# The first tile of an attention and two-expert-layer kernel: its distances, bias and operand parts cut into what the first scores read and the rest

## The chip, the cores and the metric

The kernel runs on one core of one Trainium2 chip. The metric is the device time of one execution in microseconds (us). The engines are named as the profile names them: PE (TensorE matmul), PEld (its weight loads), DVE (VectorE), ACT (ScalarE), POOL (GpSimd) and SP (SyncE, which issues the transfers here).

## What is computed

Attention over 2 batches, 8 heads, 768 positions and head size 64, then two layers of experts over the 1536 rows that come out. The part that matters here is the attention:

```python
scores = scale * np.matmul(q, k.transpose(0, 1, 3, 2))
is_global = pos[None, :] < int(n_global)            # 8
is_local = (rel >= 0) & (rel < int(n_local))        # 96, rel = row - column
keep = is_global | is_local
dist = np.where(is_global & ~is_local, float(n_local), np.abs(rel))
bias = -slopes[:, None, None] * dist[None, :, :]
scores = np.where(keep, scores + bias[None], -1e9)
a = np.exp(scores - max); a = a / (sum + 1e-9)
return np.matmul(a, v)
# then: top-1 of 8 experts (moe), then a mixture of 4 experts (moe2)
```

A row attends to at most 96 positions behind it and to the 8 global ones, so a tile of 128 rows needs its own 128 columns and those of the tile ahead of it.

## The kernel before

**Tiles and units.** The 1536 rows are 12 tiles of 128. A unit `u` is one tile with four of its eight heads, so there are 24 units; tile 0 is units 0 and 1. The loop over `u` (L483) runs several stages of different units in one turn: `stage_qk(u + 2)` (the scores on PE), `stage_e(u + 1)` (exponentials on ACT), `stage_t(u)` (transposes on PE), `stage_s(u + 2)` (scores plus bias and the row minimum on DVE, tiles `sc0x`, `sc1x`, ...), `stage_pv(u - 1)` (weights times values on PE). The order on each engine is the order of the code (`manual_schedule`); nothing is reordered.

**High and low parts.** A float32 product is made of three fp32r matmuls: high by high, high by low, low by high. So each tile's q and k get a high part (`xq00x` or `xq10x`, `kh`) by a copy on ACT (on POOL for `kh` from tile 2 on), and a low part (`xq01x` or `xq11x`, `kl`) by a subtraction in the helper `sub_lo` (L68), on POOL for q, on DVE for k of tiles 0 and 1. `prep_q`, `prep_k` do this for whole tiles of 512 columns. `save_gk` copies the global keys (`gk`) on POOL.

**Distances and bias.** `rel`, `key` and `far` are bf16 scratch rows of 640 columns inside the tile `xr` (the profile calls them `xr`): columns 0 to 511 serve tiles with a tile ahead of them, columns 512 to 639 serve a first tile, which has only its own 128 columns. POOL fills them (L135 to L142). DVE makes the distance from them with four instructions (L306 to L309) once the two integers `nints` have landed, and `make_bias` multiplies it by each head's slope (L330): first columns 512 to 639 for 8 heads, then, in the turn `u == -1`, columns 0 to 511 for 8 heads.

**PE's accumulators and fillers.** The scores of a unit take two of three PSUM tiles in turn: unit 0 `pa2x` and `pa3x`, unit 1 `sps` and `pa2x`, unit 2 `pa3x` and `sps`, unit 3 `pa2x` and `pa3x`. A unit's scores can be written when `stage_s` has read what stood there before. `warm` puts filler matmuls on a zero tile ahead of the first four units' scores, 2, 6, 6 and 6 of them, behind the 24 of L315.

**Transfers.** SP issues the loads in the order of the code: `nints`, the q half and the k half of tile 0 (`qk0x`), tile 1 (`qk1x`), small ones, then tile 2 into `qk0x` when its last reader is done.

Of the kernel before, what the change touches and what calls it, by code (L numbers as in the profile page):

```python
# [8 lines left out]
F32 = mybir.dt.float32  # L9
# [4 lines left out]
AF = mybir.ActivationFunctionType  # L14
ALU = mybir.AluOpType
# [24 lines left out]
FAR = float(4 * NOVF)  # L40
BIG = float(2 ** 38)
# [3 lines left out]
def attention_moe_moe(ctx: ExitStack, tc: tile.TileContext, qkv, nints_d, wg, w1, w2, dprob, u1, u2, out):  # L45
    nc = tc.nc
# [6 lines left out]
    cp = ctx.enter_context(tc.tile_pool(name="cp", bufs=1))  # L53
# [13 lines left out]
    def sub_lo(eng, lo, src, hi):  # L67
        eng.tensor_tensor(out=lo, in0=src, in1=hi.bitcast(F32), op=ALU.subtract)  # L68
# [50 lines left out]
    xq = [[wxp.tile([P, ND, P], F32R, name=f"xq{n}{m}x") for m in range(2)] for n in range(2)]  # L119
# [9 lines left out]
    ident = cp.tile([P, P], F32, name="ident")  # L129
# [1 line left out]
    xr = cp.tile([P, NT, D], F32, name="xr")  # L131
    nc.vector.memset(xr[:, NT - 1, :], 0.0)
    rel, key, far = (xr[:, n, :].bitcast(BF16)[:, 0:W] for n in range(NT - 4, NT - 1))
    for c, n, step, off in ((512, 1, 0, 0), (0, 2, 256, P)):
        nc.gpsimd.iota(rel[:, c:c + n * 256 - (P if n == 1 else 0)], pattern=[[0, n], [-1, 256 if n == 2 else P]], base=off, channel_multiplier=1,  # L135
                       allow_small_or_imprecise_dtypes=True)
        nc.gpsimd.iota(key[:, c:c + n * 256 - (P if n == 1 else 0)], pattern=[[0, n], [1, 256 if n == 2 else P]], base=0, channel_multiplier=0,
                       allow_small_or_imprecise_dtypes=True)
    for c in (512, 128, 384):
        nc.gpsimd.affine_select(out=rel[:, c:c + P], in_=rel[:, c:c + P], pattern=[[-1, P]], compare_op=ALU.is_ge, fill=1024.0,  # L140
                                base=0, channel_multiplier=1)
    nc.gpsimd.memset(rel[:, 256:256 + GMAX], 1024.0)  # L142
    rowf = cp.tile([P, 1], F32, name="rowf")
    nc.gpsimd.iota(rowf, pattern=[[0, 1]], base=0, channel_multiplier=1, allow_small_or_imprecise_dtypes=True)
    colf = cp.tile([P, 256], F32, name="colf")
    nc.gpsimd.iota(colf, pattern=[[1, 256]], base=0, channel_multiplier=0, allow_small_or_imprecise_dtypes=True)
    make_identity(nc, ident)
    tri = cp.tile([P, P], BF16, name="tri")
    ones = cp.tile([P, P], BF16, name="ones")
    nc.vector.memset(ones, 1.0)  # L150
    base = cp.tile([P, E1], F32, name="base")
# [134 lines left out]
        sub_lo(nc.vector, lo, src, hi)  # L286

    qkr = [lp.tile([P, 2, 512], F32, name=f"qk{j}x") for j in range(2)]
    for c in range(2):
        nc.sync.dma_start(qkr[0][:, c], qkv[0, :, c])  # L290
    load_qk(1)
    nc.sync.dma_start(wgt, wg)
# [5 lines left out]
    nval = cp.tile([P, 2], F32, name="nval")  # L298
    nc.vector.scalar_tensor_tensor(out=nval, in0=neg, scalar=float(2 ** 32), in1=nf[:, :, 0], op0=ALU.mult, op1=ALU.add)
    ngv, nlv = nval[:, 0:1], nval[:, 1:2]  # L300
    okt = cp.tile([P, 2], F32, name="okt")
    nc.vector.tensor_scalar(out=okt[:, 0:1], in0=nlv, scalar1=1.0, scalar2=None, op0=ALU.is_ge)
    nc.vector.scalar_tensor_tensor(out=okt[:, 1:2], in0=nlv, scalar=float(P - GMAX + 1), in1=okt[:, 0:1], op0=ALU.is_le, op1=ALU.mult)
    bad = cp.tile([P, 2], F32, name="bad")
    nc.vector.scalar_tensor_tensor(out=bad[:, 0:1], in0=ngv, scalar=float(GMAX), in1=okt[:, 1:2], op0=ALU.is_le, op1=ALU.mult)
    nc.vector.tensor_scalar(out=far, in0=rel, scalar1=nlv, scalar2=BIG, op0=ALU.is_ge, op1=ALU.mult)  # L306
    nc.vector.tensor_scalar(out=key, in0=key, scalar1=ngv, scalar2=BIG, op0=ALU.is_ge, op1=ALU.mult)
    nc.vector.tensor_tensor(out=rel, in0=far, in1=rel, op=ALU.max)
    nc.vector.scalar_tensor_tensor(out=rel, in0=key, scalar=nlv, in1=rel, op0=ALU.max, op1=ALU.min)  # L309
    nc.vector.tensor_scalar(out=tri, in0=colf[:, 0:P], scalar1=rowf, scalar2=None, op0=ALU.is_gt)  # L310
    nc.vector.tensor_scalar(out=base, in0=colf[:, 0:E1], scalar1=float(P), scalar2=-FAR, op0=ALU.mult, op1=ALU.add)
    with tc.tile_pool(name="ps_w", bufs=1, space=PSUM) as ps_w:
        wt = ps_w.tile([P, 256], F32, name="wt")
        for n in range(NWARM):
# [2 lines left out]
    with ExitStack() as c2:  # L317
# [7 lines left out]
        a3 = c2.enter_context(tc.tile_pool(name="a3", bufs=4))  # L325
        bias = bp.tile([P, H, W], BF16, name="bias")

        def make_bias(c):
            for h in range(H):
                nc.vector.tensor_scalar(out=bias[:, h, c], in0=rel[:, c], scalar1=-8.0 * 2.0 ** -(h + 1), scalar2=None, op0=ALU.mult)  # L330

        kh = bp.tile([P, 3, NPAIR, P], F32R, name="kh")
# [26 lines left out]
        def prep_q(t):  # L359
            qs[t] = qh, ql = xq[t % 2]  # L360
            raw = qkr[t % 2][:, 0].rearrange("p (d t) -> p d t", d=NPAIR)
            nc.scalar.activation(out=qh, in_=raw, func=AF.Copy)
            sub_lo(nc.gpsimd, ql, raw, qh)

        def prep_k(t):
            so = t % 3
            raw = qkr[t % 2][:, 1].rearrange("p (d t) -> p d t", d=NPAIR)
            if t < 2:
                nc.scalar.activation(out=kh[:, so], in_=raw, func=AF.Copy)
            else:  # L370
                copy_g(kh[:, so], raw)
            sub_lo(nc.vector if t < 2 else nc.gpsimd, kl[:, so], raw, kh[:, so])

        def save_gk(t):
            so = t % 3
# [4 lines left out]
        def load_v(t):  # L380
            nc.sync.dma_start(vv[:, t % 4, :, 0:HD], qkv[t, :, 2].rearrange("p (h e) -> p h e", h=H))
# [92 lines left out]

        NU = 2 * NT
        load_v(0)
        nc.gpsimd.memset(vv[:, :, :, HD:HV], 1.0)
        prep_q(0)
        prep_k(0)
        save_gk(0)  # L480
        load_qk(2)
        make_bias(slice(512, 640))
        for u in range(-2, NU + 5):  # L483
            t, g = divmod(u, 2)
            if u < 2:
                warm(WARMS[u + 2])
            if u + 2 < NU:
                stage_qk(u + 2)
            if 0 <= u - 2 < NU:
                run(norm(u - 2))  # L490
            if g == 0:
                if 0 <= t - 2 < NT:
                    run(rts[t - 2]["steps"][0])
                if t + 1 < NT and t >= 0:
                    load_v(t + 1)
                if t in (0, NI):
                    load_gv(t)
# [112 lines left out]
    with ExitStack() as c2:  # L610
# [76 lines left out]
        for e in range(E1 - 1):  # L687
# [17 lines left out]
            hs = hidden(pl, mp)  # L705
# [460 lines left out]
```

## Time and profile before

| | |
|---|---|
| median of 3 runs | 754.18 us (754.17 to 754.35) |
| the profiled execution: its own time, its span | 756.36 us, 754.6 us |
| PE busy over the span | 736.4 us, 98% |
| DVE, ACT, POOL busy | 522.1 us (69%), 312.7 us (41%), 252.8 us (33%) |
| granted TensorE clock, mean | 0.984 |
| first scores on DVE (unit 0), first of unit 2, first of unit 3 | 10.88 us, 17.09 us, 19.25 us |

The span runs from the first to the last instruction; 1.8 us of the profiled execution lie around it. A share of busy time is a mean over stages: in the first 20 us, which is where the change lies, PE waits for DVE, and afterwards PE has work almost without a gap. The granted clock is a share of full speed (2.4 GHz): 0.50 is the lower of its two levels, 1.2 GHz.

### The profile page before, as it was taken

What the parts mean: (1) busy time and instruction counts of PE and PEld (TensorE: products, weight loads), DVE (VectorE), ACT (ScalarE), POOL (GpSimd) and SP (SyncE); (2) the same over time, 40 slices, a digit from 0 to 9 for tenths busy, and PEclk for the clock granted to TensorE, in tenths of its full rate; (3) what the DMA queues carried; (4) which work ended last, traced back from release to release, by engine and by line L of the source; (5) the groups of instructions that cost most, each with busy time, mean ns of one, the idle gap of its engine ahead of it and who ended that gap; (6) DMA issues with size and microseconds to landing.
All of it is one profiled execution on the core that took longest, in us unless ns stands there. A gap on an engine that the chain in (4) does not pass through costs nothing.

```text
span 754.6 us, 12189 instructions
## 1 busy us (share of the span) xinstructions
PE 736.4 (98%) x4794; PEld 657.3 (87%) x4794; DVE 522.1 (69%) x1024; ACT 312.7 (41%) x489; POOL 252.8 (33%) x244
## 2 busy tenths in 40 slices
PE   8999998999999999999999999999999999999996
PEld 7999997777777898899999999999999999999995
DVE  7777863678769888576666666676666666666665
ACT  4878861687855544513223132232222322213110
POOL 5666631000046604724414244141341523415000
PEclk8999996999999999999999999999999999999999
DMA  6867602999931300200001000010000100011013
GB/s 163 277 220 247 215 21 86 387 364 405 342 103 54 99 16 28 84 29 29 29 29 56 29 29 29 29 56 29 30 29 29 56 28 29 34 38 43 1 43 129
DMA packets 36018, 74.87 MB, mean 99 GB/s; under 512 B 15960, under 2 KB 16216, under 8 KB 35954
## 3 DMA queue, kind: packets, MB, share of 16 engines
q1 hardware_dynamic: 34034, 69.39, 26.7%
q0 software_dynamic: 1920, 4.64, 1.9%
q8 instruction: 39, 0.64, 0.3%
q14 instruction: 25, 0.20, 0.1%
HBM read 65.19 MB, written 10.49 MB: 100 GB/s over the span
## 4 chain that ended last, share of the span: by engine, by line
PE 87%; DVE 5%; DMA 3%; issue 2%; ACT 2%; POOL 0%; POOLq 0%; ACTq 0%; DVEq 0%
PE pf L110 6%; PE pf L109 6%; PE pf L111 6%; PE pg L109 4%; PE pg L110 4%; PE pg L111 4%; PE pa0x L111 3%; PE pa0x L109 3%; PE pa1x L110 3%; PE pa0x L110 3%; PE pa1x L109 3%; PE pa3x L109 3%; PE pa3x L111 3%; PE pa1x L111 3%; PE pa3x L110 3%; PE pa2x L111 3%
## 5 line engine op out<-in xcount | busy, mean ns | idle before, releaser
L914 DVE TENSOR_TENSOR cc<-pg,sf 128x768 f32<-128x768 f32 x48 | 45.9, 957 | 57.0 <-PE pg L111 55.6
L896 ACT ACTIVATE sf<-pf 128x768 f32<-128x768 f32 x48 | 39.0, 813 | 107.5 <-PE pf L111 107.5
L938 ACT ACTIVATE hh0x<-cc 128x1024 fp32r<-128x1024 f32 x24 | 25.5, 1060 | 120.5 <-DVE cc L923 117.8
L938 ACT ACTIVATE hh1x<-cc 128x1024 fp32r<-128x1024 f32 x23 | 24.4, 1060 | 106.6 <-DVE cc L923 106.6
L599 POOL TENSOR_TENSOR w6x<-w4x 128x256 f32<-128x256 f32 x8 | 9.4, 1178 | 175.1 <-DMA w4x<-in_u_dram 93.2
L923 DVE TENSOR_TENSOR cc<-cc,uv 128x768 f32<-128x768 f32 x47 | 52.5, 1117 | 1.6
L939 DVE SCALAR_TENSOR_TENSOR hl0x<-cc,hh0x 128x1024 fp32r<-128x1024 f32 x24 | 29.5, 1231 | 24.8 <-ACT hh0x L938 24.8
L939 DVE SCALAR_TENSOR_TENSOR hl1x<-cc,hh1x 128x1024 fp32r<-128x1024 f32 x23 | 28.5, 1241 | 25.0 <-ACT hh1x L938 25.0
L897 DVE TENSOR_TENSOR uv<-pf,sf 128x256 f32<-128x256 f32 x48 | 20.4, 424 | 34.1 <-ACT sf L896 34.1
L110 PE MATMUL pf<-xl,r8x 128*128 128x256 f32 x144 | 40.8, 283 | 2.7 <-DVE xl L68 2.5
L857 DVE SCALAR_TENSOR_TENSOR xr<-pa2x,pr,xr 128x512 f32<-128x512 f32 x44 | 33.0, 750 | 13.4 <-PE pa2x L111 13.4
L109 PE MATMUL pf<-xh,r8x 128*128 128x256 f32 x144 | 40.6, 282 | 0.0
L111 PE MATMUL pf<-xh,r6x 128*128 128x256 f32 x144 | 40.4, 281 | 0.0
L109 PE MATMUL pf<-xh,r14x 128*128 128x256 f32 x144 | 40.4, 281 | 0.0
L110 PE MATMUL pf<-xl,r14x 128*128 128x256 f32 x144 | 40.4, 281 | 0.0
L111 PE MATMUL pf<-xh,r12x 128*128 128x256 f32 x144 | 40.4, 281 | 0.0
L599 POOL TENSOR_TENSOR w12x<-w10x 128x256 f32<-128x256 f32 x8 | 8.9, 1119 | 92.6 <-DMA w10x<-in_u_dram 92.6
L857 DVE SCALAR_TENSOR_TENSOR xr<-pa1x,pr,xr 128x512 f32<-128x512 f32 (+1 forms) x46 | 33.9, 737 | 2.2 <-PE pa1x L111 2.2
L857 DVE SCALAR_TENSOR_TENSOR xr<-pa0x,pr,xr 128x512 f32<-128x512 f32 (+1 forms) x46 | 33.9, 736 | 1.2 <-PE pa0x L111 1.2
L857 DVE SCALAR_TENSOR_TENSOR xr<-pa3x,pr,xr 128x512 f32<-128x512 f32 x45 | 33.5, 744 | 0.6 <-PE pa3x L111 0.6
L110 PEld LDWEIGHTS pf<-xl,r8x 128*128 128x128 f32 x144 | 27.0, 188 | 3.4 <-issue 2.5
L68 POOL TENSOR_TENSOR r11x<-w11x,r15x 128x1024 fp32r<-128x1024 f32 x7 | 17.0, 2424 | 35.8 <-ACT r15x L97 35.8
(1189 smaller groups left out, 2700.2 us busy)
## 6 DMA issues: line engine op xcount, KB each, us to landing
w4x<-in_u_dram SPq DMA_DIRECT2D x8, 512.0 KB, 3.2
w5x<-in_u_dram SPq DMA_DIRECT2D x8, 512.0 KB
w10x<-in_u_dram SPq DMA_DIRECT2D x8, 512.0 KB, 3.9
w11x<-in_u_dram SPq DMA_DIRECT2D x8, 512.0 KB, 3.4
qk1x<-in_qkv_dram SPq DMA_DIRECT2D x6, 512.0 KB, 4.7
vv<-in_qkv_dram SPq DMA_DIRECT2D x12, 256.0 KB, 4.9
out_dram<-xr SPq DMA_DIRECT2D x11, 256.0 KB, 2.0
qk0x<-in_qkv_dram SPq DMA_DIRECT2D x5, 512.0 KB, 4.2
```

The lines of the kernel that those rows point to most:

```text
L68: eng.tensor_tensor(out=lo, in0=src, in1=hi.bitcast(F32), op=ALU.subtract)
L109: nc.tensor.matmul(o, ah, bh, start=start, stop=False)
L110: nc.tensor.matmul(o, ah, bl, start=False, stop=False)
L111: nc.tensor.matmul(o, al, bh, start=False, stop=stop)
L599: eng.tensor_tensor(out=sm[:, 0], in0=a21, in1=a22, op=ALU.add)
L857: nc.vector.scalar_tensor_tensor(out=acc[:, tt, cs], in0=ac[:, cs], scalar=pr[:, tt, e:e + 1], in1=acc[:, tt, cs], op0=ALU.mult, op1=ALU.add)
L896: nc.scalar.activation(out=sf, in_=pf[:, 0:3], func=AF.Copy)
L897: tt(out=uv, in0=pf[:, 3], in1=sf[:, 0], op=ALU.add)
L914: tt(out=cc[:, 0:3], in0=pg, in1=sf, op=ALU.add)
L923: tt(out=cc[:, 1:4], in0=cc[:, 1:4], in1=uv.unsqueeze(1).to_broadcast([P, 3, 256]), op=ALU.add)
L938: nc.scalar.activation(out=hh, in_=cc, func=AF.Relu)
L939: nc.vector.scalar_tensor_tensor(out=hl, in0=cc, scalar=0.0, in1=hh.bitcast(F32), op0=ALU.max, op1=ALU.subtract)
```

## The change

It reorders and cuts up the work of tile 0; the sum of what is computed stays. (1) POOL fills columns 512 to 639 first, then makes `ident`, then the other columns. (2) The k half of tile 0 is loaded ahead of the q half. (3) The four distance instructions become a function `window(c)`, called for columns 512 to 639 ahead of the first scores and for columns 0 to 511 in the turn `u == -1`. (4) `prep_first` makes the high and low parts of tile 0 in two halves of two head pairs: for the first half the low parts of k and q are subtracted on DVE, for the second half both on POOL. (5) The bias of columns 512 to 639 is made for heads 0 to 3 ahead of the first scores and for heads 4 to 7 behind them. (6) Five small instructions (`okt`, `bad`, `tri`, `base`) move behind the first scores.

```diff
-    for c, n, step, off in ((512, 1, 0, 0), (0, 2, 256, P)):
...
-    for c in (512, 128, 384):
+    iotas(512, 1)
+    past_only(512)
+    make_identity(nc, ident)
...
-    make_identity(nc, ident)
+    iotas(0, 2)
+    for c in (128, 384):
+        past_only(c)
...
-    for c in range(2):
+    for c in (1, 0):
         nc.sync.dma_start(qkr[0][:, c], qkv[0, :, c])
...
+    def window(c):
+        nc.vector.tensor_scalar(out=far[:, c], in0=rel[:, c], scalar1=nlv, scalar2=BIG, op0=ALU.is_ge, op1=ALU.mult)
+        nc.vector.tensor_scalar(out=key[:, c], in0=key[:, c], scalar1=ngv, scalar2=BIG, op0=ALU.is_ge, op1=ALU.mult)
+        nc.vector.tensor_tensor(out=rel[:, c], in0=far[:, c], in1=rel[:, c], op=ALU.max)
+        nc.vector.scalar_tensor_tensor(out=rel[:, c], in0=key[:, c], scalar=nlv, in1=rel[:, c], op0=ALU.max, op1=ALU.min)
...
-        def make_bias(c):
-            for h in range(H):
+        def make_bias(c, hs=range(H)):
+            for h in hs:
...
+        def prep_first():
+            raws = [qkr[0][:, n].rearrange("p (d t) -> p d t", d=NPAIR) for n in (1, 0)]
+            qs[0] = xq[0]
+            for d in (slice(0, 2), slice(2, 4)):
+                eng = nc.gpsimd if d.start else nc.vector
+                parts = [(kh[:, 0, d], kl[:, 0, d], raws[0][:, d]), (xq[0][0][:, d], xq[0][1][:, d], raws[1][:, d])]
+                for hi, _, raw in parts:
+                    nc.scalar.activation(out=hi, in_=raw, func=AF.Copy)
+                for hi, lo, raw in parts:
+                    sub_lo(eng, lo, raw, hi)
...
         load_v(0)
+        window(slice(512, 640))
         nc.gpsimd.memset(vv[:, :, :, HD:HV], 1.0)
-        prep_q(0)
-        prep_k(0)
+        prep_first()
+        make_bias(slice(512, 640), range(4))
         save_gk(0)
         load_qk(2)
-        make_bias(slice(512, 640))
...
             if u == -2:
+                make_bias(slice(512, 640), range(4, H))
+                small_constants()
                 prep_q(1)
...
             if u == -1:
+                window(slice(0, 512))
                 make_bias(slice(0, 512))
```

What stands on DVE ahead of the first scores (`sc0x`), behind `nval` (the two integers as floats), in the kernel before:

```order
L302 TENSOR_SCALAR okt<-nval 128x1
L303 SCALAR_TENSOR_TENSOR okt<-nval,okt 128x1
L305 SCALAR_TENSOR_TENSOR bad<-nval,okt 128x1
L306 TENSOR_SCALAR xr<-xr,nval 128x640
L307 TENSOR_SCALAR xr<-xr,nval 128x640
L308 TENSOR_TENSOR xr<-xr 128x640
L309 SCALAR_TENSOR_TENSOR xr<-xr,nval 128x640
L310 TENSOR_SCALAR tri<-colf,rowf 128x128
L311 TENSOR_SCALAR base<-colf 128x8
L68 TENSOR_TENSOR kl<-qk0x,kh 128x512
L330 TENSOR_SCALAR bias<-xr 128x128 x8
L418 ISA sc0x,mn<-pa2x,bias 128x128
```

and in the change:

```order
L311 TENSOR_SCALAR xr<-xr,nval 128x128
L312 TENSOR_SCALAR xr<-xr,nval 128x128
L313 TENSOR_TENSOR xr<-xr 128x128
L314 SCALAR_TENSOR_TENSOR xr<-xr,nval 128x128
L68 TENSOR_TENSOR kl<-qk0x,kh 128x256
L68 TENSOR_TENSOR xq01x<-qk0x,xq00x 128x256
L342 TENSOR_SCALAR bias<-xr 128x128 x4
L442 ISA sc0x,mn<-pa2x,bias 128x128
```

Five small instructions, four of eight bias instructions and the 512 other columns have left this place; half of the q subtraction has come to it.

What stands on DVE from the last scores of unit 1 (`sc1x`) to the first of unit 2 (`sc2x`), in the kernel before:

```order
L418 ISA mn 128x1
L418 ISA sc1x,mn<-pa2x,bias 128x128
L418 ISA mn 128x1
L330 TENSOR_SCALAR bias<-xr 128x512 x8
L418 ISA sc2x,mn<-pa3x,bias 128x256
```

and in the change:

```order
L442 ISA mn 128x1
L311 TENSOR_SCALAR xr<-xr,nval 128x512
L312 TENSOR_SCALAR xr<-xr,nval 128x512
L313 TENSOR_TENSOR xr<-xr 128x512
L314 SCALAR_TENSOR_TENSOR xr<-xr,nval 128x512
L342 TENSOR_SCALAR bias<-xr 128x512 x8
L442 ISA sc2x,mn<-pa3x,bias 128x256
```

The four distance instructions of the 512 columns now stand ahead of unit 2's scores. Between the scores of units 0 and 1 DVE has, besides the subtraction of tile 1's `kl` that was there, four bias instructions and the five small ones. So all that left the place ahead of `sc0x` stands ahead of `sc2x` still.

POOL's subtractions and copies for tiles 0, 1 and 2, in the kernel before (`qk0x` holds tile 0, then tile 2):

```order
L68 TENSOR_TENSOR xq01x<-qk0x,xq00x 128x512
L378 TENSOR_SCALAR gk<-kh 128x128
L378 TENSOR_SCALAR gk<-kl 128x128
L68 TENSOR_TENSOR xq11x<-qk1x,xq10x 128x512
L357 TENSOR_SCALAR kh<-qk0x 128x512
L68 TENSOR_TENSOR kl<-qk0x,kh 128x512
L68 TENSOR_TENSOR xq01x<-qk0x,xq00x 128x512
```

and in the change:

```order
L68 TENSOR_TENSOR kl<-qk0x,kh 128x256
L68 TENSOR_TENSOR xq01x<-qk0x,xq00x 128x256
L402 TENSOR_SCALAR gk<-kh 128x128
L402 TENSOR_SCALAR gk<-kl 128x128
L68 TENSOR_TENSOR xq11x<-qk1x,xq10x 128x512
L369 TENSOR_SCALAR kh<-qk0x 128x512
L68 TENSOR_TENSOR kl<-qk0x,kh 128x512
L68 TENSOR_TENSOR xq01x<-qk0x,xq00x 128x512
```

One subtraction of 512 columns has become two of 256. PE's matmuls stand in the same order in both.

## Rows read from the trace of the kernel before

**Rows 1.** The page: granted TensorE clock in 40 slices of the span, in tenths.
```profile
PEclk8999996999999999999999999999999999999999
```

**Rows 2.** Timeline of DVE: start, duration, instruction, idle before it and who ended that.
```profile
4.47 0.15 DVE L302 TENSOR_SCALAR okt<-nval 128x1 f32<-128x1 f32 x1
...
4.93 0.38 DVE L306 TENSOR_SCALAR xr<-xr,nval 128x640 bf16<-128x640 bf16 x1
...
5.52 1.58 DVE L308 TENSOR_TENSOR xr<-xr 128x640 bf16<-128x640 bf16 x1
7.13 0.89 DVE L309 SCALAR_TENSOR_TENSOR xr<-xr,nval 128x640 bf16<-128x640 bf16 x1
...
8.80 2.16 DVE L330 TENSOR_SCALAR bias<-xr 128x128 bf16<-128x128 bf16 x8
10.88 0.28 DVE L418 CUSTOM_DVE_ANT_0 sc0x<-pa2x,bias 128x128 f32<-128x128 f32 x1
...
11.72 0.68 DVE L68 TENSOR_TENSOR kl<-qk1x,kh 128x512 fp32r<-128x512 f32 x1
13.04 0.29 DVE L418 CUSTOM_DVE_ANT_0 sc1x<-sps,bias 128x128 f32<-128x128 f32 x1 [0.63 <-PE sps L407]
...
13.89 3.28 DVE L330 TENSOR_SCALAR bias<-xr 128x512 bf16<-128x512 bf16 x8
17.09 0.41 DVE L418 CUSTOM_DVE_ANT_0 sc2x<-pa3x,bias 128x256 f32<-128x256 f32 x1
```

**Rows 3.** Timeline of POOL.
```profile
5.47 1.28 POOL L68 TENSOR_TENSOR xq01x<-qk0x,xq00x 128x512 fp32r<-128x512 f32 x1 [1.33 <-ACT xq00x L362]
...
8.97 0.42 POOL L378 TENSOR_SCALAR gk<-kl 128x128 fp32r<-128x128 f32 x1 [1.71 <-DVE kl L68]
9.36 1.34 POOL L68 TENSOR_TENSOR xq11x<-qk1x,xq10x 128x512 fp32r<-128x512 f32 x1
12.53 0.62 POOL L357 TENSOR_SCALAR kh<-qk0x 128x512 fp32r<-128x512 f32 x1 [1.83 <-DMA qk0x<-in_qkv_dram]
...
14.47 1.33 POOL L68 TENSOR_TENSOR xq01x<-qk0x,xq00x 128x512 fp32r<-128x512 f32 x1
```

**Rows 4.** The tile `bias`, 8.5 to 11 us: count, duration ns min/median/max.
```profile
L330 DVE TENSOR_SCALAR bias<-xr x8: 181/188/1303, 8.8 to 10.8; 128x128 bf16<-128x128 bf16 x8
```

**Rows 5.** Timeline of DVE, the second of the eight bias instructions of 512 columns.
```profile
14.60 1.36 DVE L330 TENSOR_SCALAR bias<-xr 128x512 bf16<-128x512 bf16 x1
```

**Rows 6.** Timeline of ACT.
```profile
4.75 0.63 ACT L362 ACTIVATE xq00x<-qk0x 128x512 fp32r<-128x512 f32 x1 [2.52 <-DMA qk0x<-in_qkv_dram]
5.42 0.63 ACT L369 ACTIVATE kh<-qk0x 128x512 fp32r<-128x512 f32 x1
```

**Rows 7.** Timeline of SP's transfers.
```profile
8.95 0.34 SPq L276 DMA_DIRECT2D qk0x<-in_qkv_dram  x1
```

**Rows 8.** Timeline of PE: first scores of unit 0, second matmul of unit 3.
```profile
6.95 0.32 PE L407 MATMUL pa2x<-kh,xq00x 64*128 64x128 f32 x1
...
18.25 0.38 PE L407 MATMUL pa3x<-kh,xq10x 64*128 64x256 f32 x1
```

**Rows 9.** Busy time by stretch: length, each engine (count), granted clock, DMA share, GB/s.
```profile
7.00:8.90 1.90, 0.27 (x3) 0.13 (x2) 1.86 (x6) 1.02 (x2) 0.26 (x1) 1.00 0.28 42
...
10.20:11.60 1.40, 1.11 (x5) 0.69 (x3) 1.40 (x10) 0.40 (x2) 0.50 (x1) 0.50 0.70 260
11.60:13.10 1.50, 1.46 (x11) 1.35 (x11) 0.87 (x4) 0.92 (x5) 0.57 (x1) 0.50 0.16 63
13.10:16.90 3.80, 3.80 (x22) 3.34 (x22) 3.80 (x16) 1.76 (x5) 2.62 (x3) 0.50 0.90 229
17.00:47.00 30.00, 30.00 (x296) 28.33 (x295) 22.09 (x122) 23.95 (x55) 18.98 (x28) 1.00 0.83 252
```

**Rows 10.** Busy time by stretch at the end of the attention.
```profile
109.10:112.50 3.40, 2.57 (x25) 2.57 (x24) 1.50 (x11) 1.13 (x3) 1.75 (x3) 1.00 0.05 15
...
122.80:126.20 3.40, 3.40 (x19) 3.34 (x19) 0.76 (x6) 0.00 (x0) 1.19 (x2) 0.50 0.04 15
```

More of the change, by code (lines that the diff above doesn't have):

```diff
@@ L133, in attention_moe_moe, with iotas, past_only @@
     rel, key, far = (xr[:, n, :].bitcast(BF16)[:, 0:W] for n in range(NT - 4, NT - 1))
-    for c, n, step, off in ((512, 1, 0, 0), (0, 2, 256, P)):
[L135 to L138, printed above, removed]
-    for c in (512, 128, 384):
+    def iotas(c, n):
+        w = 256 if n == 2 else P
+        for a, step, off, ch in ((rel, -1, P if n == 2 else 0, 1), (key, 1, 0, 0)):
+            nc.gpsimd.iota(a[:, c:c + n * w], pattern=[[0, n], [step, w]], base=off, channel_multiplier=ch, allow_small_or_imprecise_dtypes=True)
+    def past_only(c):
         nc.gpsimd.affine_select(out=rel[:, c:c + P], in_=rel[:, c:c + P], pattern=[[-1, P]], compare_op=ALU.is_ge, fill=1024.0,
                                 base=0, channel_multiplier=1)
-    nc.gpsimd.memset(rel[:, 256:256 + GMAX], 1024.0)
+    iotas(512, 1)
+    past_only(512)
+    make_identity(nc, ident)
     rowf = cp.tile([P, 1], F32, name="rowf")
@@ L146, in attention_moe_moe @@
     nc.gpsimd.iota(colf, pattern=[[1, 256]], base=0, channel_multiplier=0, allow_small_or_imprecise_dtypes=True)
-    make_identity(nc, ident)
+    iotas(0, 2)
+    for c in (128, 384):
+        past_only(c)
+    nc.gpsimd.memset(rel[:, 256:256 + GMAX], 1024.0)
     tri = cp.tile([P, P], BF16, name="tri")
@@ L300, in attention_moe_moe, with small_constants @@
     ngv, nlv = nval[:, 0:1], nval[:, 1:2]
-    okt = cp.tile([P, 2], F32, name="okt")
-    nc.vector.tensor_scalar(out=okt[:, 0:1], in0=nlv, scalar1=1.0, scalar2=None, op0=ALU.is_ge)
-    nc.vector.scalar_tensor_tensor(out=okt[:, 1:2], in0=nlv, scalar=float(P - GMAX + 1), in1=okt[:, 0:1], op0=ALU.is_le, op1=ALU.mult)
     bad = cp.tile([P, 2], F32, name="bad")
[L305 to L311, printed above, removed]
+    def window(c):
[3 more added lines that the diff above has]
+        nc.vector.scalar_tensor_tensor(out=rel[:, c], in0=key[:, c], scalar=nlv, in1=rel[:, c], op0=ALU.max, op1=ALU.min)
+    def small_constants():
+        okt = cp.tile([P, 2], F32, name="okt")
+        nc.vector.tensor_scalar(out=okt[:, 0:1], in0=nlv, scalar1=1.0, scalar2=None, op0=ALU.is_ge)
+        nc.vector.scalar_tensor_tensor(out=okt[:, 1:2], in0=nlv, scalar=float(P - GMAX + 1), in1=okt[:, 0:1], op0=ALU.is_le, op1=ALU.mult)
+        nc.vector.scalar_tensor_tensor(out=bad[:, 0:1], in0=ngv, scalar=float(GMAX), in1=okt[:, 1:2], op0=ALU.is_le, op1=ALU.mult)
+        nc.vector.tensor_scalar(out=tri, in0=colf[:, 0:P], scalar1=rowf, scalar2=None, op0=ALU.is_gt)
+        nc.vector.tensor_scalar(out=base, in0=colf[:, 0:E1], scalar1=float(P), scalar2=-FAR, op0=ALU.mult, op1=ALU.add)
     with tc.tile_pool(name="ps_w", bufs=1, space=PSUM) as ps_w:
```

## Prediction

> **What bounds the kernel now.** I looked first at what PE does, since it is busy 98% of the span, and in which stretches that is not true. The table by stretch shows it: from 17 to 47 us PE has 30.00 of 30 us of work, but from 7.0 to 8.9 us only 0.27 of 1.90 [rows 9]. So the fill of the pipeline, up to some 18 us, is the only part that the change touches, and whatever PE gets there earlier or later is carried behind it. What PE waits for in the fill is read from two places. Its first scores start at 6.95 us; the second matmul of unit 3 starts at 18.25 us [rows 8], and it needs `pa3x`, which DVE frees when it has read unit 2's heads 0 and 2. DVE starts on unit 2 at 17.09 us, straight behind the eight bias instructions of 512 columns [rows 2]. From 18.25 us on PE never waits for long. **So unit 2's scores on DVE, not unit 0's, are the gate of the fill**, and the question is where DVE comes to them.
>
> **What DVE does until then.** From 4.47 to 17.09 us are 12.62 us, and much of it is not work. A bias instruction of 128 columns takes 188 ns, but one takes 1303 ns [rows 4]; it is the one that runs while POOL subtracts `xq11x` (9.36 to 10.70 us). The TENSOR_TENSOR at 5.52 us takes 1.58 us and ends 0.35 us after POOL's `xq01x` (5.47 to 6.75 us); the second wide bias instruction takes 1.36 us beside POOL's third subtraction (14.47 to 15.80 us) [rows 2, 3, 5]. The eight narrow ones need 0.10 us each without that, from start to start, and took 2.08 us. So a DVE instruction that meets a two-input subtraction on POOL stands until POOL is through. The Trainium skill, page "SBUF — State Buffer", section "Who interferes with whom", has this as a lock on a port pair that VectorE and GpSimd share: whichever issues first keeps the other out for the whole instruction. The trace agrees, with 1303 ns against 188; by that rule unit 2 starts where the sum below has it, and if the three long instructions were chance, it would start where the second rival has it.
>
> **The change on DVE, step by step.** The unhindered prices, start to start, from [rows 2, 4, 5]: a distance TENSOR_SCALAR of 640 columns 0.30 us (two from 4.93 to 5.52), so some 0.13 and 0.25 for 128 and 512; the TENSOR_TENSOR 0.35 us at 640 (its part behind POOL), so 0.2 and 0.35 with a wait for its input; the SCALAR_TENSOR_TENSOR is 0.89 us long, so 0.25 and 0.67 without its end, which the next overlaps. A narrow bias 0.10; a wide one 0.20 (the last six of eight between 15.96 and 17.09). A subtraction of 512 columns 0.68, so of 256 about 0.4. Four scores of 128 columns 0.84 (10.88 to 11.72).
>
> (a) *Ahead of unit 0's scores.* The four narrow distance instructions take from 4.47 to about 5.2 us. ACT has the k half at 4.75 us [rows 6]; half of 0.63 us and its fixed part give 0.4, so `kh` is there at 5.2 and DVE has half of `kl` at 5.6. The q half now lands second; before, the second half was first read at 5.42, which I take for its landing, the latest that it can have been [rows 6]. Half of `xq00x` is then ready at 5.8, DVE's half of `xq01x` at 6.25. POOL's two halves, 0.66 us each (half of 1.28), run from 6.2 to 7.5 and hold up DVE's four bias instructions, which need 0.4, to about 7.8. PE's fillers still end at 6.95 [rows 8], its 12 matmuls of unit 0 need 0.9 (0.10 each for the 296 of the stretch from 17 us, and these are narrow [rows 9]), so unit 0's scores start on DVE at **7.85 us instead of 10.88**. This part does what it says.
>
> (b) *Between units 0 and 1.* DVE ends unit 0 at 8.7. POOL: 7.5, two copies of `gk` at 0.4 each, `xq11x` from 8.35 to 9.7 (1.34) [rows 3]. The other four bias instructions come at 8.7, right into it: they end at 10.0, not 9.1. Then `okt`, `bad`, `tri`, `base` 0.7 (0.46 for three of them, from 4.47 to 4.93 [rows 2], and as much again for half as many), then tile 1's `kl` 0.6 to 0.7: unit 1 starts at 11.35 (13.04 before, with a wait of 0.63 for PE that is gone) and ends at 12.2.
>
> (c) *Ahead of unit 2.* Tile 2's load was issued at 8.95 and POOL started on it at 12.53, 3.58 us later [rows 3, 7]. It is now issued behind POOL's halves, at 7.6, so POOL copies `kh` from 11.2 and subtracts `kl` and `xq01x` from 11.9 to 14.5. The four wide distance instructions come at 12.2, into these two: one of them slips in between, the second stands until 14.5. Then 0.15 for its rest, 0.35, 0.67 and 8 x 0.20 for the bias: **unit 2 starts at 17.2 us, where it starts now (17.09)**. As a balance: 12.62 us before held 4.6 us of standing (1.2 at 5.52, 1.2 in the narrow bias, 1.6 in the wide, 0.63 for PE); after it is 12.7 with 4.1 to 4.4 of standing, since two-fold fixed parts of the split distances (0.3), one more subtraction of 256 columns (0.1) and a wait for q's half (0.3) have come. Bounds: 16.6 if tile 2's load lands 0.5 us sooner, 17.7 if both wide distances stand twice.
>
> **PE and its clock.** PE's order does not change. It ends unit 0 at 7.85, runs six fillers, unit 1 by 9.5, six fillers, one matmul of unit 2; the next needs `sps`, free when DVE has read unit 1, at 12.1. Unit 2 and the transposes of unit 0 end at 13.7, six fillers at 14.4 (a little later at a lower clock), and then PE has nothing until `pa3x` is free, 1.15 us behind unit 2's start: **18.35 us**. Before, the fillers and unit 2 filled this time; now PE stands 2 us and then some 4. The granted clock tells what such a gap costs. It was 1.00 until PE stood in the stretch 7.0 to 8.9 us, then 0.50 (1.2 GHz) in all of 10.2 to 16.9 us, although PE was busy again: 1.46 of 1.50 us from 11.6 to 13.1 did not bring it back, 3.80 of 3.80 from 13.1 to 16.9 did [rows 9]. That half-speed stretch cost nothing, for DVE was the gate. After a longer gap PE will meet unit 3 at half speed, and there PE itself is the gate. It stays so for between 3.8 us (13.1 to 16.9) and 5.3 us (11.6 to 16.9) of dense work; I take the upper one, since the stretch from 11.6 counted for nothing. At half speed half of that is lost: 1.9 to 2.65 us, taken as **2.6**. By instructions per us it would be less (22 in 3.8 against 296 in 30, so 41% lost, 1.6 to 2.2), but the fillers in the first are longer ones.
>
> **What lies behind.** From 18 us on the other engines wait on PE or on what PE released, and loads are issued in the same order, so the delay is passed on whole. One more place depends on time: the page shows a second half-speed slice [rows 1], from 112.5 to 126.2 us, behind a stretch in which PE was busy 2.57 of 3.40 us and ending behind one with 3.40 of 3.40 [rows 10]. Its start and end can fall on other work if all is 2.7 us later. If the start moves with the work, nothing changes (taken: 0); bounds are -0.3 and +2.0, half of up to 4 us more of work at half speed. POOL's new order of iotas costs nothing: it ended at 4.1 us, 1.33 us ahead of its first subtraction [rows 3], and DVE asks for the distances at 4.47 at the earliest. The load order of q and k costs nothing but the 0.3 us in (a).
>
> **The sum.** Unit 2 +0.1, half-speed stretch +2.6, the rest 0: +2.7 us. On the profiled execution, span 754.6 and own time 756.36, this makes 757.3 and 759.1; on the median of the three runs, 754.18, it makes **756.9 us**.
>
> **The rivals.** I call 0.2% (1.5 us) about what a measurement of this kernel can tell from no change.
>
> *No difference, 753.0 to 755.6 us, chance 0.20.* PE's gap is as I say but the clock is back sooner, or unit 2 comes 1 to 2 us sooner and pays for a part of the loss. It decides if the half-speed stretch behind 18 us is under 3 us. For it speaks that such a stretch cost nothing before; against it, that the clock stayed low for 6.7 us [rows 9]. Central: 754.3.
>
> *Faster, 750.2 to 752.6 us, chance 0.17.* POOL does not stop DVE as I sum it: the narrow instructions of (b) and the wide ones of (c) pass. Without any standing unit 2 would start at 13.1, 4.0 us sooner, PE's gap would be short enough not to matter, and the time 750.2; with half of it, 752.2. It decides if unit 2 starts before about 15.5 us. Against it speak three instructions with 1.2 us and more over their price [rows 2, 4, 5], and that POOL's subtractions follow right where DVE's new work stands.
>
> *Slower, the forecast, 755.7 to 758.6 us, chance 0.53; more, 758.6 to 760, chance 0.10*, where the second half-speed stretch grows as well, by up to 2.0 us.
>
> **How the numbers follow.** Faster 0.17, same 0.20, slower 0.63. The likeliest case gives 756.9, its own range is 755.7 to 758.6. To leave out no more than 2 in 10, I go down into the case of no difference, to 753.4, which leaves out faster, and up to 759.0.
>
> **What would show it.** Right: first scores of unit 0 at 7.9 us; a narrow bias instruction of about 1 us beside POOL's `xq11x`; a wide distance instruction of over 1 us beside POOL's `kl` or `xq01x`; unit 2's scores between 16.6 and 17.7; PE idle for over 3 us ahead of unit 3 with the clock at 0.50 behind it, to 22 or 24 us; then every stage of PE later by a fixed 2 to 3 us. Wrong: unit 2 before 15.5 us, or the clock at 1.00 from 18 us on.

## The result and the profile after

The changed kernel takes 758.92 us (median of 11 executions, 757.34 to 763.35), the kernel before 754.35 (11 executions): ratio 1.0061, 95% interval [1.0047, 1.0076], slower. The forecast was 756.9. The same kernel measured again later gave 757.65 against 755.30, ratio 1.0018 [0.9993, 1.0043], which by itself cannot be told from no change (run e7 below). A ratio given here with its interval is not the quotient of the two medians, which would be 1.0031 for that run. The profiled execution of the change took 758.03 us, its span 756.1.

The page after, busy time and granted clock:

```profile
PE 735.9 (97%) x4794; PEld 657.0 (87%) x4794; DVE 523.3 (69%) x1029; ACT 313.5 (41%) x491; POOL 252.5 (33%) x245
...
PEclk9899997999999999999999999999999999999999
```

The sums hardly move, as they must: nearly the same work in another order. The second digit has gone from 9 to 8 [rows 1]: PE is slower between 18.9 and 37.8 us, where before it was at full speed. (The first has gone from 8 to 9: the clock of 0.50 that lasted from 10.2 to 16.9 us [rows 9] now lasts from 12 to 15 us. The seventh, from 6 to 7, is the tail, told below.) The timeline of DVE says how the fill got there:

```profile
6.14 1.79 DVE L342 TENSOR_SCALAR bias<-xr 128x128 bf16<-128x128 bf16 x4
7.85 0.28 DVE L442 CUSTOM_DVE_ANT_0 sc0x<-pa2x,bias 128x128 f32<-128x128 f32 x1
...
8.69 1.06 DVE L342 TENSOR_SCALAR bias<-xr 128x128 bf16<-128x128 bf16 x4
...
10.98 0.28 DVE L442 CUSTOM_DVE_ANT_0 sc1x<-sps,bias 128x128 f32<-128x128 f32 x1
...
11.82 0.35 DVE L311 TENSOR_SCALAR xr<-xr,nval 128x512 bf16<-128x512 bf16 x1
12.09 1.37 DVE L312 TENSOR_SCALAR xr<-xr,nval 128x512 bf16<-128x512 bf16 x1
13.38 1.49 DVE L313 TENSOR_TENSOR xr<-xr 128x512 bf16<-128x512 bf16 x1
14.90 0.75 DVE L314 SCALAR_TENSOR_TENSOR xr<-xr,nval 128x512 bf16<-128x512 bf16 x1
15.69 1.71 DVE L342 TENSOR_SCALAR bias<-xr 128x512 bf16<-128x512 bf16 x8
17.31 0.42 DVE L442 CUSTOM_DVE_ANT_0 sc2x<-pa3x,bias 128x256 f32<-128x256 f32 x1
```

Compare it with [rows 2]. Unit 0's scores start 3.03 us sooner, unit 1's 2.06 us sooner, unit 2's 0.22 us later: the lead is used up on the way. Where, the timeline of POOL shows:

```profile
6.16 0.77 POOL L68 TENSOR_TENSOR kl<-qk0x,kh 128x256 fp32r<-128x256 f32 x1 [2.07 <-ACT kh L394]
6.88 0.73 POOL L68 TENSOR_TENSOR xq01x<-qk0x,xq00x 128x256 fp32r<-128x256 f32 x1
...
8.12 1.26 POOL L68 TENSOR_TENSOR xq11x<-qk1x,xq10x 128x512 fp32r<-128x512 f32 x1
...
11.96 1.35 POOL L68 TENSOR_TENSOR kl<-qk0x,kh 128x512 fp32r<-128x512 f32 x1
13.27 1.32 POOL L68 TENSOR_TENSOR xq01x<-qk0x,xq00x 128x512 fp32r<-128x512 f32 x1
```

Lay the two beside each other. The second wide distance instruction (12.09) ends 0.15 us behind POOL's `kl`, the third (13.38) 0.28 us behind POOL's `xq01x`. Together they take 2.8 us from start to start. What PE then does is in its timeline:

```profile
18.48 0.39 PE L431 MATMUL pa3x<-kh,xq10x 64*128 64x256 f32 x1 [2.63 <-DVE mn L442]
...
22.52 0.58 PE L431 MATMUL sps<-kh,xq00x 64*128 64x256 f32 x1
...
26.65 0.38 PE L431 MATMUL sps<-kh,xq00x 64*128 64x256 f32 x1
```

and in the table by stretch (length, then busy time and count of PE, PEld, DVE, ACT, POOL, then the granted clock):

```profile
10.40:11.70 1.30, 0.31 (x1) 0.11 (x1) 1.30 (x9) 0.41 (x1) 0.44 (x1) 1.00 0.11 41
11.80:15.50 3.70, 3.70 (x22) 3.32 (x22) 3.67 (x6) 2.06 (x7) 2.70 (x3) 0.54 0.92 231
15.50:18.40 2.90, 0.35 (x2) 0.15 (x1) 2.87 (x16) 0.63 (x2) 0.00 (x0) 1.00 0.92 240
18.70:25.50 6.80, 6.80 (x42) 6.23 (x41) 3.49 (x20) 3.85 (x10) 3.66 (x5) 0.50 0.63 171
...
117.70:128.00 10.30, 9.15 (x45) 8.29 (x44) 3.25 (x22) 0.60 (x1) 2.38 (x4) 0.50 0.11 42
```

PE starts unit 3's second matmul at 18.48 us, 0.23 later than before [rows 8]. That alone would be nothing. But ahead of it PE had 0.35 us of work in 2.90, and from 18.7 to 25.5 us the granted clock is 0.50: 42 instructions in 6.8 us, where full speed gave 296 in 30 [rows 9], some 67 in 6.8. Unit 5's scores start on PE at 26.65 us, 23.36 before: 3.3 us later. At the end of the attention the second matmul group of the tile `xtp` of one output tile starts at 112.91 us, 109.94 before, so 3.0 are still there. PE's timeline in the kernel before (unit 5, `xtp`, the first matmul of the expert layers), then in the change:

```profile
23.36 0.38 PE L407 MATMUL sps<-kh,xq00x 64*128 64x256 f32 x1
...
109.94 0.44 PE L281 MATMUL xtp<-ident,xr 128*128 128x128 f32 x2 [0.83 <-DVE xr L465]
...
127.40 0.50 PE L109 MATMUL pa0x<-r16x,xq00x 128*128 128x512 f32 x1 [0.74 <-ACT xq00x L285]
```

```profile
112.91 0.44 PE L287 MATMUL xtp<-ident,xr 128*128 128x128 f32 x2 [0.83 <-DVE xr L489]
...
128.94 0.50 PE L109 MATMUL pa0x<-r16x,xq00x 128*128 128x512 f32 x1 [0.74 <-ACT xq00x L291]
```

The profiled spans differ by 1.5 us only. The first matmul of the expert layers (L109) follows that `xtp` row after 16.03 us in the change, 17.46 in the profile of before, since the second half-speed stretch there was longer: 13.6 us (112.6 to 126.2) against 10.3. The profiles of e1 to e9 below have 15.83 to 16.04. Among them is e9, which is the kernel before with other fillers: it comes to that row at 110.05 us, 0.11 later than the kernel before, and has 16.04. So the long stretch is taken as scatter of the kernel before, of which there is one profile, and not as a gain of the change.

### The profile page after: what moved, and what is told of

It reads as the page before. It is cut to its first block, busy times and chain, and to the rows that moved or that the text cites. A ratio compares the mean times of both kernels' runs of the same rounds, so it can differ in the third digit from the quotient of the medians.

```text
span 756.1 us, 12199 instructions
## 1 busy us (share of the span) xinstructions
PE 735.9 (97%) x4794; PEld 657.0 (87%) x4794; DVE 523.3 (69%) x1029; ACT 313.5 (41%) x491; POOL 252.5 (33%) x245
## 4 chain that ended last, share of the span: by engine, by line
PE 88%; DVE 4%; issue 2%; DMA 2%; ACT 1%; POOL 0%; POOLq 0%; ACTq 0%; DVEq 0%
PE pf L110 6%; PE pf L109 6%; PE pf L111 6%; PE pg L109 4%; PE pg L111 4%; PE pg L110 4%; PE pa0x L111 3%; PE pa0x L109 3%; PE pa0x L110 3%; PE pa1x L111 3%; PE pa1x L109 3%; PE pa1x L110 3%; PE pa3x L109 3%; PE pa3x L111 3%; PE pa3x L110 3%; PE pa2x L109 3%
## 5 line engine op out<-in xcount | busy, mean ns | idle before, releaser
L965 ACT ACTIVATE hh0x<-cc 128x1024 fp32r<-128x1024 f32 x24 | 25.5, 1061 | 120.5 <-DVE cc L950 120.5
L109 PE MATMUL pf<-xh,r8x 128*128 128x256 f32 x144 | 40.5, 282 | 0.0
L109 PE MATMUL pf<-xh,r14x 128*128 128x256 f32 x144 | 40.4, 281 | 0.0
```

The lines of the kernel that those rows point to most:

```text
L109: nc.tensor.matmul(o, ah, bh, start=start, stop=False)
L965: nc.scalar.activation(out=hh, in_=cc, func=AF.Relu)
```

## The experiments

Theory A is the prediction's: unit 2's scores on DVE are the gate; the narrow work that left the front stands ahead of them still, where POOL's subtractions stop it; and the gap that PE now has ahead of unit 3 costs the loss, by half speed over dense work. Rivals: the time is lost elsewhere (load order, split instructions, the tail); or DVE is slow there for a reason other than POOL. e1 to e4 were measured on one chip, e5 to e7 on another, e8 and e9 each on one of its own, always beside the kernel before; each has 12 executions, but e4 has 6 and e8 has 5. The change itself was measured in the first comparison and in e7 only.

**e1: the change, with the gap filled.** More filler matmuls ahead of units 1, 2 and 3, 48 in all (the expectation says 46):

```diff
-WARMS = (2, 6, 6, 6)
+WARMS = (2, 8, 18, 40)
```

> The change with 46 more filler matmuls on PE (8, 18 and 40 ahead of units 1, 2 and 3 in place of 6 each), nothing else. Theory: the change is slower because PE stands ahead of unit 3 and the clock is at 0.50 when unit 3 comes; with PE kept busy the clock stays at 1.00 from 18 us on, unit 2's scores on DVE still start at 17.2 to 17.4 us, and the time is that of the kernel before within 1.5 us, 3 to 4.5 us under the change. Rival (the loss comes from the new order on DVE, POOL and the transfers, the clock is a bystander): the time stays within 1.5 us of the change, or is longer by up to 4 us, since 40 fillers take 4.3 us at full speed and 8.5 at half.

754.57 us against 755.21: ratio 1.0001 [0.9976, 1.0025]. The timeline of DVE, that of PE (units 3 and 5), and the table by stretch:

```profile
17.41 0.42 DVE L442 CUSTOM_DVE_ANT_0 sc2x<-pa3x,bias 128x256 f32<-128x256 f32 x1
```

```profile
18.58 0.38 PE L431 MATMUL pa3x<-kh,xq10x 64*128 64x256 f32 x1
...
23.69 0.38 PE L431 MATMUL sps<-kh,xq00x 64*128 64x256 f32 x1
```

```profile
15.50:18.40 2.90, 2.90 (x24) 2.65 (x22) 2.87 (x14) 0.53 (x2) 0.00 (x0) 1.00 0.91 309
18.70:25.50 6.80, 6.80 (x71) 6.26 (x72) 5.31 (x29) 6.36 (x17) 4.39 (x8) 1.00 0.59 146
```

Units 2 and 3 come as late as in the change, a little later even, but the clock stays at 1.00, 71 matmuls pass in the 6.8 us where 42 did, and unit 5 starts on PE at 23.69 us, not at 26.65 (23.36 before). The loss is gone, within the 2 us that the interval leaves to either side. Load order and split instructions are still in this kernel, so they cost no more than that.

**e2: the kernel before, with a gap.** Its fillers ahead of units 1, 2 and 3 are taken away:

```diff
-WARMS = (2, 6, 6, 6)
+WARMS = (2, 0, 0, 0)
```

> The kernel before without the 18 fillers ahead of units 1, 2 and 3. Theory: nothing is moved on DVE or POOL, but PE stands for 1 to 2 us more ahead of unit 3, so the clock does not come back at 17 us and unit 3 and what follows run at 0.50 for 3 to 7 us: slower than before by 1.5 to 3.5 us, with unit 2's scores on DVE still at 17.1 us or a little earlier. Rival: the fillers only take PE's time; without them the time is the same or up to 1 us shorter.

757.98 us, ratio 1.0041 [1.0025, 1.0058]. Unit 2 on DVE, unit 3's second matmul and unit 5 on PE, from their timelines, and the table by stretch:

```profile
17.11 0.41 DVE L418 CUSTOM_DVE_ANT_0 sc2x<-pa3x,bias 128x256 f32<-128x256 f32 x1
```

```profile
18.28 0.58 PE L407 MATMUL pa3x<-kh,xq10x 64*128 64x256 f32 x1 [1.51 <-DVE mn L418]
...
26.68 0.38 PE L407 MATMUL sps<-kh,xq00x 64*128 64x256 f32 x1
```

```profile
18.70:25.50 6.80, 6.80 (x42) 6.23 (x41) 3.43 (x18) 3.65 (x10) 3.66 (x5) 0.50 0.83 247
```

DVE and unit 3 stand where they stood [rows 2, 8], yet the first matmul takes 0.58 us instead of 0.38, the clock is 0.50 from 8.6 to 25.6 us, unit 5 starts at 26.68 us as in the change (26.65), and the loss is of the size of the change's. So idle time of PE in the fill makes it, without any of the change's edits. Which of PE's waits it takes is not separated: e1 and e2 each alter the fillers ahead of three units at once, and in e2 the clock was down long before the wait ahead of unit 3, which is 1.51 us here.

**e3: the change, with POOL's two subtractions for tile 2 cut short.** It leaves out most of tile 2's low parts: 8 of 128 columns of each head pair are subtracted, `kl` is zeroed once.

```diff
-            sub_lo(nc.gpsimd, ql, raw, qh)
+            part = slice(0, 8) if t == 2 else slice(0, P)
+            sub_lo(nc.gpsimd, ql[:, :, part], raw[:, :, part], qh[:, :, part])
...
-            sub_lo(nc.vector if t < 2 else nc.gpsimd, kl[:, so], raw, kh[:, so])
+            part = slice(0, 8) if t == 2 else slice(0, P)
+            sub_lo(nc.vector if t < 2 else nc.gpsimd, kl[:, so, :, part], raw[:, :, part], kh[:, so, :, part])
```

> The change, with POOL's two subtractions for tile 2 (kl and xq01x) cut from 512 to 32 columns; the low parts of the other columns are left out (zero, or what tile 0 left there). Theory: the wide distance instructions on DVE stand only because POOL subtracts; now the second takes some 0.3 us for 1.37 and the third 0.4 for 1.49, unit 2's scores start at 15.0 to 15.4 us instead of 17.3, and the time falls by 2 us or more, 2.2 for the gate and up to 3 for a shorter gap on PE. Rival (those two instructions are long by themselves): they keep 1.3 to 1.5 us, unit 2's scores stay at 17.3, the time stays within 1 us of the change.

755.99 us, ratio 0.9999 [0.9978, 1.0021]. The timelines of DVE and of PE:

```profile
12.46 0.34 DVE L312 TENSOR_SCALAR xr<-xr,nval 128x512 bf16<-128x512 bf16 x1
12.72 0.41 DVE L313 TENSOR_TENSOR xr<-xr 128x512 bf16<-128x512 bf16 x1
...
15.58 0.42 DVE L444 CUSTOM_DVE_ANT_0 sc2x<-pa3x,bias 128x256 f32<-128x256 f32 x1
```

```profile
16.75 0.38 PE L433 MATMUL pa3x<-kh,xq10x 64*128 64x256 f32 x1 [2.14 <-DVE mn L444]
```

The same two instructions fall from 1.37 and 1.49 to 0.34 and 0.41 us with nothing on DVE changed: what they stood for was POOL. Unit 2 comes 1.73 us sooner. But PE still has a gap of 2.14 us, the clock is 0.50 from 17.5 to 24.3, unit 4's scores start at 20.40 (20.59 before), unit 5's at 24.95 (23.36 before), and the gain is eaten: no difference from before. Against the two medians of the change, which were taken on other occasions, it is 1.7 and 2.9 us less, where 2 or more was expected.

**e4: the change, with only what unit 2 reads ahead of unit 2.** Columns 0 to 255 of the distances and heads 0 to 3 of their bias come ahead of unit 1's scores, the rest behind units 2 and 3:

```diff
             if u == -2:
                 make_bias(slice(512, 640), range(4, H))
-                small_constants()
...
-            if u == -1:
-                window(slice(0, 512))
-                make_bias(slice(0, 512))
+                window(slice(0, 256))
+                make_bias(slice(0, 256), range(4))
+            if u == 0:
+                make_bias(slice(0, 256), range(4, H))
+                small_constants()
+            if u == 1:
+                window(slice(256, 512))
+                make_bias(slice(256, 512))
```

> The change, but ahead of unit 2's scores only what units 1 and 2 read: the distances of columns 0 to 255 and the bias of those for heads 0 to 3 stand ahead of unit 1's scores; heads 4 to 7 and the five small instructions stand behind unit 2's, columns 256 to 511 behind unit 3's. Theory: the gate is unit 2's place on DVE; it starts at 13 to 14 us, PE has no long gap, and the time is 2 to 4 us under the kernel before, 6 to 8 under the change. Rival (the transfers of tiles 2 and 3 or POOL's parts gate unit 3 and 4 next): unit 2 is early, the gain over the kernel before is under 1.5 us.

761.19 us, ratio 1.0080 [1.0054, 1.0106]: slower, which was not expected. The timelines of DVE and of PE:

```profile
11.75 3.16 DVE L342 TENSOR_SCALAR bias<-xr 128x256 bf16<-128x256 bf16 x4
...
22.67 1.19 DVE L311 TENSOR_SCALAR xr<-xr,nval 128x256 bf16<-128x256 bf16 x1
```

```profile
15.60 0.58 PE L431 MATMUL sps<-kh,xq10x 64*128 64x256 f32 x1 [4.89 <-DVE mn L442]
```

Four bias instructions took 3.16 us, since they fell into POOL's tile 2 subtractions (from 12.35 and 13.56 us), now *ahead of* unit 1; eight of twice the width took 1.71 us in the change. PE stood 4.89 us; later the other distances met tile 3's subtractions. The clock was 0.50 from 11.5 to 21.8 and from 28.6 to 32.0 us. The mechanism held and my placing was wrong: less work, put where POOL subtracts, takes longer than more work put elsewhere.

**e5: the change, with tile 2's subtractions on DVE, behind unit 2's scores.** POOL then has nothing that stops DVE ahead of the gate; the fillers cover PE. The load of tile 4, which needs their input read, is issued behind them.

```diff
-WARMS = (2, 6, 6, 6)
+WARMS = (2, 8, 18, 24)
...
-            sub_lo(nc.gpsimd, ql, raw, qh)
+            if t == 2:
+                late.append(lambda: sub_lo(nc.vector, ql, raw, qh))
+            else:
+                sub_lo(nc.gpsimd, ql, raw, qh)
...
+            if u == 0:
+                run(late)
+                load_qk(4)
```

(`kl` likewise.)

> The change with more fillers (8, 18 and 24) and with tile 2's two low parts subtracted on DVE behind unit 2's scores, not on POOL (tile 4's load is then issued behind them). Theory: no wide distance instruction stands any more, unit 2's scores start at 15.2 to 15.7 us, the clock stays at 1.00; unit 3's scores on DVE then wait behind 1.3 us of subtractions, so PE is ahead of the kernel before by 1 to 2 us from unit 4 on: 1 to 2 us under the kernel before, 4 to 6 under the change. Rival (POOL's lock only moves the wait to DVE's own work): unit 4 on PE starts where it does before, the time is that of the kernel before within 0.8 us.

753.27 us against 755.30, ratio 0.9959 [0.9932, 0.9987]: faster than both kernels. The timelines of DVE and of PE:

```profile
12.08 0.35 DVE L312 TENSOR_SCALAR xr<-xr,nval 128x512 bf16<-128x512 bf16 x1
12.35 0.42 DVE L313 TENSOR_TENSOR xr<-xr 128x512 bf16<-128x512 bf16 x1
...
15.21 0.42 DVE L450 CUSTOM_DVE_ANT_0 sc2x<-pa3x,bias 128x256 f32<-128x256 f32 x1
...
17.19 0.68 DVE L68 TENSOR_TENSOR xq01x<-qk0x,xq00x 128x512 fp32r<-128x512 f32 x1
17.79 0.41 DVE L450 CUSTOM_DVE_ANT_0 sc3x<-pa2x,bias 128x256 f32<-128x256 f32 x1
```

```profile
18.71 0.38 PE L439 MATMUL sps<-kh,xq00x 64*128 64x256 f32 x1
...
21.73 0.38 PE L439 MATMUL sps<-kh,xq00x 64*128 64x256 f32 x1
```

Unit 2 comes 2.10 us sooner than in the change. On PE unit 4 starts 1.88 us and unit 5 1.63 us sooner than before, and the medians lie 2.0 apart. e1 had more fillers alone and gained nothing, so the gain goes with the new place of the subtractions. The subtraction that POOL needs 1.32 us for takes DVE 0.68. It is not quite free there: unit 3's scores start on DVE 2.58 us behind unit 2's, 2.16 before.

**e6: the change, with the wide bias of heads 4 to 7 behind unit 2's scores**, and fillers to match:

```diff
-WARMS = (2, 6, 6, 6)
+WARMS = (2, 8, 18, 32)
...
-                make_bias(slice(0, 512))
+                make_bias(slice(0, 512), range(4))
+            if u == 0:
+                make_bias(slice(0, 512), range(4, H))
```

> The change with more fillers (8, 18 and 32) and with the wide bias of heads 4 to 7 made behind unit 2's scores. Theory: unit 2's scores start 0.8 us sooner (four times 0.20), at 16.5 us, POOL does nothing then, so nothing stands; PE is 0.6 to 0.8 us ahead of the kernel before from unit 3 on: 0 to 1.5 us under the kernel before. Rival: unit 3's scores wait for the four instructions instead, the time is that of the first experiment, no gain over the kernel before.

753.65 us, ratio 0.9969 [0.9940, 0.9999]. Unit 2 starts at 16.59 us, unit 4 on PE at 20.09 (20.59 before), the clock stays at 1.00. It is faster, at the edge of what the interval separates.

**e7: the change again, as it is.**

> The change as it is, beside the others on the same chip. Theory: the fill makes unit 5 on PE 3.2 us later, and what lies behind, the second half-speed stretch included, is the same on the mean: 2.5 to 4 us over the kernel before. Rival: the second half-speed stretch, at the end of the attention, is longer too and makes 4 to 6 us of it.

757.65 us against 755.30, ratio 1.0018 [0.9993, 1.0043]: by the time alone no difference is shown, and the 2.35 us between the medians fall just short of the 2.5 to 4 expected. The trace still has the loss. Unit 3's second matmul in the timeline of PE:

```profile
18.55 0.58 PE L431 MATMUL pa3x<-kh,xq10x 64*128 64x256 f32 x1 [4.17 <-DVE mn L442]
```

DVE comes to unit 2 at 17.39, as in the first profile (17.31), but the half-speed stretch is 16.6 to 26.8 us here; unit 4 starts at 22.77 (22.52 there) and unit 5 at 27.38 (26.65 there, 23.36 before). From 12 to 15 us, where the first profile has 0.50, the clock is 1.00 here, so the fillers end sooner and PE stands 4.17 us, not 2.63. From `xtp` to L109 are 15.84 us, so the rival's longer second stretch is not there. Place and kind repeat; the size is not one number, as the stretch starts and ends elsewhere in each execution.

**e8: the kernel before, with more fillers**, to see whether its own half-speed stretch from 10.2 to 17.0 us costs anything:

```diff
-WARMS = (2, 6, 6, 6)
+WARMS = (20, 6, 12, 34)
```

> The kernel before with more fillers (20, 6, 12 and 34 ahead of units 0 to 3), nothing else. Theory: its half-speed stretch from 10 to 17 us cost nothing, since DVE is the gate; with the clock at 1.00 all through the fill, unit 2's scores still start at 16.8 to 17.2 us and the time is that of the kernel before within 1 us. Rival (the clock of the fill costs the kernel before too): 2 us or more under it.

758.50 us against 754.22, ratio 1.0059 [1.0045, 1.0072]. The expectation missed by more than 3 us. The timeline of PE and the end of unit 2's scores on DVE:

```profile
16.86 4.32 PE L345 MATMUL ov1x<-wz 128*128 128x256 f32 x34
21.10 0.38 PE L407 MATMUL pa2x<-kh,xq10x 64*128 64x256 f32 x1
```

```profile
18.57 0.08 DVE L418 DVE_READ_ACCUMULATOR2_ANT mn<- 128x1 f32 x1
```

DVE has finished unit 2 at 18.65, but PE is in its 34 fillers until 21.10 and so comes to unit 3 some 2.9 us later than before [rows 8]: I had given the fillers too much room. Unit 5 is 2.8 us late on PE (26.20 us); the trace does not show the rest of the 4.3 between the medians. Nor did they keep the clock up: it was 0.57 from 12 to 16 us, so the question went unanswered.

**e9: the same with 12 instead of 34 ahead of unit 3.**

```diff
-WARMS = (20, 6, 12, 34)
+WARMS = (20, 6, 12, 12)
```

> The kernel before, with 20 filler matmuls ahead of unit 0's scores as in the last run, but 12 instead of 34 ahead of unit 3's. Theory A (the last run's 4.3 us came from too many fillers: its 34 ran from 16.86 to 21.10 us, past the end of the softmax that unit 3 waits for, at about 18.3 us, so they themselves pushed unit 3 back 2.85 us): at the 0.127 us that one of them took, 12 end at about 18.4, unit 3's scores start at 18.25 to 18.6 us, unit 4's at 20.6 to 20.9, and the median comes within 1 us of the kernel before. Theory B (the fillers ahead of unit 0, or the half-speed stretch at a later place, cost the time): unit 3 starts near 18.3 all the same, but a later half-speed stretch over dense work gives 2 us or more back, and the median stays 3 to 5 us above before.

755.04 us against 754.71, ratio 0.9992 [0.9973, 1.0011]. The timeline of PE:

```profile
16.89 1.67 PE L345 MATMUL ov1x<-wz 128*128 128x256 f32 x12
18.49 0.38 PE L407 MATMUL pa2x<-kh,xq10x 64*128 64x256 f32 x1
```

Unit 3 starts at 18.49 and the loss is gone: it was the 22 fillers too many. The clock was 0.58 from 12 to 15 us in this run too, and that cost nothing that shows within the 2 us of the interval.

## Why the prediction was right

**The gate.** Right: unit 2's scores on DVE were forecast at 17.2 us and start at 17.31, though unit 0's come at 7.85, to the hundredth where the sum has them. The hundredth is luck: the sum has PE's matmuls of unit 0 end at 7.85, behind fillers that end at 6.95; in the trace PE starts them at 6.22 us, and it is DVE's bias instructions that last to 7.85. e3 and e5 show that unit 2 is the gate: with it sooner by 1.7 and 2.1 us, PE's second matmul of unit 3 follows (16.75 and 16.38 us, 18.48 in the change).

**DVE stands beside POOL.** Right, and shown by e3 and e5 from both sides: 1.37 and 1.49 us beside POOL's subtractions, 0.34 to 0.42 without. The narrow bias instructions lost less in (b) than I gave them (unit 1 at 10.98, not 11.35, since POOL's `xq11x` was over at 9.38 and not 9.7), and that came to nothing, as the next subtractions were waiting. In (c) I let one wide distance instruction slip through and one stand; one passed (0.35 us) before POOL began, two stood, and the sum was the same, since the standing ends with POOL's subtractions, at 14.59 us where the sum has 14.5. Not every DVE instruction stands: unit 0's scores, which read an accumulator and the bias, took 0.28 us each at 8.27 and 8.48 us, inside POOL's `xq11x`. The Trainium skill, page "SBUF — State Buffer", section "Who interferes with whom", has the port pair locked by whoever issues first, for the whole instruction, and counts among those that contend a DVE instruction with two inputs in SBUF, and a `tensor_scalar` with one where it runs in a two-port mode. The trace agrees for L313 with two inputs (1.49 us); L312 with one (1.37 us) stands as well, but no view here shows its mode.

**PE's gap and the clock.** Right in place and sign, shown by e1 and e2: fill PE's idle time in the change and the loss goes, make some in the kernel before and it comes. The mis-sized term is the half-speed stretch: I took 5.3 us of it and 2.6 of loss from before's row; it lasted 6.8 us in the profile of the change (8.1 behind 18.7 us in e7), and unit 5 came 3.3 us later, 0.2 of it from DVE. PE's gap was 2.63 us in the first profile, not the 4 that I gave it, since the clock was 0.50 there from 12 to 15 us already, which the prediction did not have; in e7, without that, it was 4.17. e3 shows that 2.14 are followed by half speed too.

**The tail.** Taken as 0, and the profile seems to say -1.4; but that is an unusually long stretch in the one profile of before. Against the 15.83 to 16.04 us from `xtp` to L109 in the profiles of e1 to e9, the tail of the change (16.03) is unchanged.

**The sum.** 2.7 us forecast; the traces give some 3.0 at the end of the attention (3.7 in e7), the medians 4.6 in one comparison and 2.4 in the other. The 4.6 is more than the fill explains. No profile shows the other 1.6 us; that a later second stretch falls on dearer work in some executions fits, but was only argued. The 758.92 us lie above the 755.7 to 758.6 of the likeliest case, in the band that the prediction gave to a longer second half-speed stretch, and neither profile of the change has one (10.3 and 10.2 us, 13.6 before). So the place, the sign and the mechanism were forecast; that the median still lies under the upper end of the range, 759.0, is luck.

## What to carry to other kernels

Making the first result sooner is worth nothing while a later wait sets the pace: follow the front of the pipeline up to the instruction from which the bounding engine never waits again, and count what still stands ahead of that one. Work moved on DVE should be laid against POOL's timeline, for it is the meeting and not the amount that costs. In this kernel a gap on PE ahead of dense work had to be covered by fillers that end when the wait ends: by the traces too few cost some 3 us, and too many (e8) as much.

## What was not expected of the hardware

A gap of little over 2 us on PE (2.14 in e3, 2.63 in the change) was followed by 6.8 us at 1.2 GHz over dense work, which cost the change some 3 us. Yet 18 more fillers ahead of unit 0 in e8 and e9, with the clock at 1.00 up to 12 us, did not keep it from 0.57 and 0.58 behind that, where PE's last wait ahead of it was 0.77 us (up to 11.64 us). And where the half-speed stretches lie differs between two executions of one kernel (12 to 15 and 18.7 to 25.6 us in the first profile, 16.6 to 26.8 in e7), with DVE at unit 2 at nearly the same time (17.31 and 17.39 us).
